# Splitting the natural-layout load of a linear-attention chunk, and moving the output's zero fill

## The chip, the cores and the metric

One Trainium2 chip, one of its cores. The metric is the device time of the kernel in microseconds (us), the median of several runs. The engines are TensorE (PE, with its weight loads as PEld), VectorE (DVE), ScalarE (ACT), GpSimd (POOL) and SyncE (SP); SP does no arithmetic and issues most of the DMAs, each when its turn in SP's queue has come and what it waits for has arrived.

## The reference

Three layers in a row, in float32. First a linear attention with a state per head (4 batches, 8 heads, 768 steps, 48 channels), then a dense layer pair on the 3072 tokens of 384 channels, then a mixture of 8 experts of which each token takes two:

```python
for t in range(S):
    cur = einsum('bhd,bhe->bhde', u * k_t, v_t)
    y[:, :, t] = einsum('bhd,bhde->bhe', r_t, state + cur)
    state = w_t[..., None] * state + einsum('bhd,bhe->bhde', k_t, v_t)
x = y as (3072, 384)
x = ((x @ w1) * (x @ w2)) @ w3 @ w_out
out = sum over the 2 best experts e: weight * (relu(x @ w1[e]) @ w2[e])
```

The term with u is, at each step and head, the sum over channels of r * k * u, times v.

## The kernel before, in words

The time axis is cut into 24 chunks of 128 steps, all eight heads at once. Each chunk has two inputs. dtc (772 KB, load_dt, line 177) holds r, k and w with channels on partitions. natc (640 KB, load_na, line 181) holds r, k and v with steps on partitions, r and k in the first 768 columns and v, padded, in the last 512. Both have two buffers, so the load for chunk j + 2 waits for the last reader of chunk j.

The thirteen steps of a chunk are the list STEPS (line 331). The ones that matter here: pre_u (line 217) makes rku = r*k*u from natc by two multiplies, on DVE for chunks 2 to 4 and on POOL for all others, into a single buffer; pre_c (line 224) sums it over the channels of a head on DVE (cc); pre_d (line 230) puts cc on a diagonal with eight ACT instructions (am); at_ov lays the products of chunk j over the rest of am; at_T turns k for the state; at_kv (line 257, from do_kv) adds k v to the state; at_y (line 278, from do_y) is the chunk's output on PE, which reads v from natc, and its two halves xh (ACT) and xl (DVE). y and the transposes of at_T share one PSUM bank (bY). After y of chunk j, do_y issues load_na(j + 2); after pre_r of chunk j, do_r issues load_dt(j + 2).

Two chunks make a group of 256 tokens, which then passes through the dense layers: mo_ab (line 486, eighteen matmuls of 256 columns a call), mo_x (line 510, twelve of 400) and mo_out. Matrices are split into a high and a low part, so each product is three matmuls (mm3, line 169). A group has 12 slots; at the end of each, run_todo issues the attention steps whose slot it is. The slots are written out by hand: chunk j takes them from WHEN (line 399) for j up to 5 and from 6j - 14 + LATE (line 405) after that. From chunk 6 on, y stands at slot 6j - 8, pre_u at 6j - 17, pre_r at 6j - 16, pre_c at 6j - 16 and pre_d at 6j - 15. Within one slot, instructions come in the order in which they were registered, loads of weights ahead of steps. Only DVE runs in the program's order; the framework orders the other engines' queues, SP's too, by its own modelled times, apart from instructions in keep_in_program_order, which stay behind what was traced before them on their engine.

At slot 14 fill_table (line 635) sets the routing table's slots to their start values by three stores of short rows and zeroes 896 rows of x2 in DRAM. At slots 24, 30, 36, 42 and 48 fill_out (line 646) zeroes one fifth of the output each, which the experts later add to by scatter.

In the slots below 0 the weights w3 and w_out are folded into one matrix (the prologue), beside the first steps of chunks 0 to 2. After the twelve groups come the eight experts, which this change doesn't touch; their loads and gathers begin in the last group.

Of the kernel before, what the change touches and what calls it, by code (L numbers as in the profile page):

```python
# [8 lines left out]
F32 = mybir.dt.float32  # L9
# [7 lines left out]
OP = mybir.AluOpType  # L17

P = 128
B, H, S, D = 4, 8, 768, 48  # L20
DM, FF, E = 384, 1024, 8
N = B * S
NCH = N // P
# [3 lines left out]
VW = 64  # L27
NDT = 8 * P + 8 * (HC + 1)
NNAT = 2 * DM + H * VW
# [8 lines left out]
NROW = N + DUMP  # L38
# [33 lines left out]
def tile_kernel(ctx: ExitStack, tc: tile.TileContext, dt, nat, w3t, wout, w1, w2, e1, e2, cf, ci, out):  # L72
    nc = tc.nc
    pe, act, dve, pool, sp = nc.tensor, nc.scalar, nc.vector, nc.gpsimd, nc.sync
# [15 lines left out]
    def c(n):  # L90
        o, w = CF[n]
        return cft[:, o:o + w]
# [21 lines left out]
    att = attx.enter_context(tc.tile_pool(name="att", bufs=2))  # L114
# [57 lines left out]
        pe.matmul(o, wl, xh, start=False, stop=stop)  # L172


    DT, NA, FG, RC, KT, RT, AM, KN, XH, XL, KS = ({} for _ in range(11))

    def load_dt(j):
        DT[j] = att.tile([P, NDT], F32, name="dtc")
        sp.dma_start(out=DT[j], in_=dt[j])

    def load_na(j):
        NA[j] = att.tile([P, NNAT], F32, name="natc")
        sp.dma_start(out=NA[j], in_=nat[j])

    def fgv(j):
        return FG[j].rearrange("p (a i) -> p a i", i=HC + 1)
# [6 lines left out]
    def pre_rec(j, step):  # L193

        fa = fgv(j)[:, :, 1:]
        if step == 0:
            RC[j] = att.tile([P, 8, HC], F32, name="rc", bufs=1)
            KT[j] = att.tile([P, 4, 2, HC], F32, name="kt")
            act.activation(out=RC[j], in_=fa, func=AF.Ln)
            act.activation(out=RC[j], in_=RC[j], func=AF.Exp, scale=-1.0)  # L200
        else:
            t = KT[j].rearrange("p a s i -> p (a s) i")
            dve.tensor_tensor(out=t, in0=fa, in1=RC[j], op=OP.mult)
            dve.scalar_tensor_tensor(RC[j], t, -2.0, RC[j], op0=OP.add, op1=OP.mult)
# [12 lines left out]
    def pre_u(j):  # L217
        t = att.tile([P, DM], F32, name="rku", bufs=1)
        on = dve if 2 <= j < 5 else pool
        on.tensor_tensor(out=t, in0=NA[j][:, :DM], in1=NA[j][:, DM:2 * DM], op=OP.mult)  # L220
        on.tensor_tensor(out=t, in0=t, in1=c("u"), op=OP.mult)
        KS["u", j] = t

# [28 lines left out]
        act.copy(out=KN[j].rearrange("p a t -> p (a t)"), in_=bY)  # L252

    def vv(j, h):
        return NA[j][:, 2 * DM + h * VW:2 * DM + (h + 1) * VW]

    def at_kv(j):
        kv = bK[:, :4 * D].rearrange("p (a e) -> p a e", a=4)
        for a in range(4):
            for hb in range(2):  # L260
                pe.matmul(kv[64 * hb:64 * hb + 64, a], KN[j][:, a, 64 * hb:64 * hb + 64],  # L261
                          vv(j, 2 * a + hb)[:, 16 * hb:16 * hb + D], start=True, stop=True,
                          tile_position=(0, 64 * hb))
        sc = att.tile([P, 4], F32, name="sc")
        dve.tensor_tensor(out=sc, in0=fgv(j)[:, 0::2, HC], in1=fgv(j + 1)[:, 1::2, HC], op=OP.mult)

        new = att.tile([P, 4, D], F32, name="snew", bufs=2)
        src = kv
        if j % CPB:
            src = att.tile([P, 4, D], F32, name="stmp", bufs=1)  # L270
            dve.tensor_tensor(out=src, in0=kv, in1=KS["s", j], op=OP.add)
        dve.tensor_tensor(out=new, in0=src, in1=sc[:, :, None].to_broadcast([P, 4, D]), op=OP.mult)
        KS["s", j + 1] = new
        for hb in range(2):
            q = slice(64 * hb, 64 * hb + D)
            act.copy(out=St[(j + 1) % 2][q, :, D * hb:D * hb + D], in_=new[q])

    def at_y(j):
        first = j % CPB == 0
        yv = bY[:, :3 * P].rearrange("p (k t) -> p k t", k=3)  # L280
        qs = []
        for q in range(4):
            lst = []
            for kb in range(3):
                a, b = PIECES[kb][q]
                if b is None:
                    hs, so = ((a, 32 * (a % 2)),), 64 * (a % 2)
                else:
                    hs, so = ((a, 32), (b, 0)), 32
                ms = [(vv(j, h)[:, o:o + 32], AM[j][:, h, :]) for h, o in hs]  # L290
                if not first:
                    ms.append((St[j % 2][:, a // 2, so:so + 32], RT[j][:, a // 2].rearrange("p s i -> p (s i)")))
                for i, (lt, rh) in enumerate(ms):
                    lst.append((yv[32 * q:32 * q + 32, kb], lt, rh, i == 0, i == len(ms) - 1, (0, 32 * q)))
            qs.append(lst)
        for i in range(max(map(len, qs))):
            for q in range(4):
                if i < len(qs[q]):
                    o, lt, rh, st, en, tp = qs[q][i]
                    pe.matmul(o, lt, rh, start=st, stop=en, tile_position=tp)  # L300
        g, s = divmod(j, 2)
        if s == 0:
            XH[g] = xp.tile([P, 3, 2 * P], F32R, name="xh")
            XL[g] = xp.tile([P, 3, 2 * P], F32R, name="xl")
        h, l = XH[g][:, :, s * P:s * P + P], XL[g][:, :, s * P:s * P + P]
        act.copy(out=h, in_=yv)  # L306
        dve.tensor_tensor(out=l, in0=yv, in1=f(h), op=OP.subtract)

    def do_y(j):
        at_y(j)  # L310
        if j + 2 < NCH:
            load_na(j + 2)

    def do_kv(j):
        if j % CPB < CPB - 1:
# [10 lines left out]
    def do_r(j):  # L326
        pre_r(j)
        if j + 2 < NCH:
            load_dt(j + 2)

    STEPS = (do_kv, do_y, at_A, do_ov, do_T, pre_scan, lambda j: pre_rec(j, 1), pre_k, do_r, lambda j: pre_rec(j, 0),
             pre_u, pre_c, pre_d)


    woh, wol = [w.rearrange("p (j d) -> p j d", d=XW) for w in (WBh, WBl)]
# [53 lines left out]
    SPG = 12  # L389
    todo = {}  # L390

    def at(slot, fn, *a):
        todo.setdefault(slot, []).append((fn, a))

    def run_todo(k):
        for fn, a in todo.pop(k, []):
# [1 line left out]

    WHEN = {0: (-13, -12, -14, -13, -14, -21, -18, -17, -17, -20, -19, -16, -14),
# [15 lines left out]
    for slot, fn, a in zip(LDA, (load_dt, load_na, load_dt, load_na), (0, 0, 1, 1)):  # L415
        at(slot, fn, a)
# [227 lines left out]
            out=x2d[:DUMP].rearrange("(a p) d -> p a d", p=P), in_=zeros[:, None, :].to_broadcast([P, NT, DM])))  # L644

    def fill_out(i):
        lo, hi = [k * (NROW // P) // 5 for k in (i, i + 1)]
        n = hi - lo
        tc.keep_in_program_order(sp.dma_start(
            out=out[lo * P:hi * P].rearrange("(a p) d -> p a d", p=P),  # L650
            in_=zeros[:, None, :].to_broadcast([P, n, DM])))
# [171 lines left out]
        gate_at(SPG * ((t0 + GB) // 2) + 3, t0, 1 + late,  # L823
                (9, 9, 9, 10, 10, 10, 11, 11) if late else (13, 14, 17, 17, 19, 20, 23, 23))
    at(SPG + 2, fill_table)
    for i in range(5):
        at(2 * SPG + 6 * i, fill_out, i)

    for g in range(NGRP):
        sub = [(mo_ab, g, 0, 0), (mo_ab, g, 0, 1), None, (mo_ab, g, 1, 0), (mo_ab, g, 1, 1), (mo_x, g, 0),  # L830
# [188 lines left out]
```

## Time and profile before

| what | value |
| --- | --- |
| median of 3 runs | 945.47 us (944.18 to 946.84) |
| the profiled execution | 945.79 us |
| its span, first to last instruction | 944.0 us |
| mean granted TensorE clock | 0.989 |
| TensorE busy | 96% of the span |
| VectorE, ScalarE, GpSimd busy | 49%, 45%, 35% |

How to read it: the span is what the rows below are laid out in, with times from its start. The prologue takes it to about 66 us, group 0 to about 113 us, the other groups to about 475 us, and the experts to the end. The granted clock is the share of TensorE's full rate of 2.4 GHz that the chip allowed. Idle time of an engine counts only if it holds up the one that bounds the stretch; who that is, the chain of waits shows: it goes from the last instruction back, at each step to what released it. A load's time to landing runs from its issue to its completion, with what it stood in line for.

### The profile page before, as it was taken

How to read it: one execution, taken by the hardware profiler on the slowest of the kernel's cores; microseconds unless marked ns; L12 is line 12 of the kernel's file. 1: busy time of each engine (PE TensorE's matmuls, PEld its weight loads, DVE VectorE, ACT ScalarE, POOL GpSimd, SP SyncE). 2: the span in 40 equal slices, each digit the busy share in tenths (PEclk: the TensorE clock that was granted, in tenths of full speed). 3: DMA queues.
4: the chain of work that ended last, by engine and by line, in shares of the span. 5: the costliest groups of instructions: out<-in, count | busy, mean ns of one | idle time of the engine just before them, and what ended most of it. 6: DMA issues, size and time to landing. Idle time of an engine off the chain costs nothing.

```text
span 944.0 us, 17811 instructions
## 1 busy us (share of the span) xinstructions
PE 909.2 (96%) x7235; PEld 843.2 (89%) x7235; DVE 461.1 (49%) x1126; ACT 422.3 (45%) x875; POOL 331.0 (35%) x267
## 2 busy tenths in 40 slices
PE   8998895999999999999999999999999999999994
PEld 6787795999999999999999989899898998989894
DVE  5888753676776866866344353231313223130320
ACT  6776533645546456455252343433424343332420
POOL 1100101023032132131414635655556564555412
PEclk9999997999999999999999999999999999999998
DMA  9944595565334244230140555335163532614112
GB/s 356 369 166 171 191 85 178 165 201 143 120 79 124 81 97 123 76 83 30 31 171 18 108 186 156 65 95 136 28 170 70 154 65 75 153 34 104 17 20 36
DMA packets 49180, 111.65 MB, mean 118 GB/s; under 512 B 17600, under 2 KB 32192, under 8 KB 49088
## 3 DMA queue, kind: packets, MB, share of 16 engines
q1 hardware_dynamic: 33472, 85.98, 29.4%
q0 software_dynamic: 12160, 19.72, 11.6%
q10 hardware_dynamic: 3456, 4.72, 1.4%
q8 instruction: 58, 0.95, 0.4%
q14 instruction: 34, 0.28, 0.1%
HBM read 88.12 MB, written 22.27 MB: 117 GB/s over the span
## 4 chain that ended last, share of the span: by engine, by line
PE 87%; DVE 4%; ACT 4%; DMA 2%; issue 1%; POOL 1%; POOLq 0%; SPq 0%; ACTq 0%; DVEq 0%
PE pb L170 26%; PE pb L171 25%; PE pb L172 25%; PE pb L300 3%; PE pb L240 2%; PE pb L726 2%; DMA natc<-nat 2%; PE pb L764 1%; PE pb L261 1%; ACT am L233 1%; PE pb L250 1%; ACT top L145 1%; DVE cvz L154 1%; DMA raw<-w 0%; DVE am L245 0%
## 5 line engine op out<-in xcount | busy, mean ns | idle before, releaser
L170 PE MATMUL pb<-XTh,WAh 128*128 128x512 f32 (+1 forms) x384 | 133.3, 348 | 0.0
L171 PE MATMUL pb<-XTl,WAh 128*128 128x512 f32 (+1 forms) x384 | 131.9, 343 | 0.0
L170 PE MATMUL pb<-WBh,HH 128*128 128x384 f32 x384 | 130.9, 341 | 0.0
L172 PE MATMUL pb<-XTh,WAl 128*128 128x512 f32 (+1 forms) x384 | 130.9, 343 | 0.0
L172 PE MATMUL pb<-WBh,HH 128*128 128x384 f32 x384 | 129.6, 337 | 0.0
L171 PE MATMUL pb<-WBl,HH 128*128 128x384 f32 x384 | 129.5, 337 | 0.0
L742 DVE SCALAR_TENSOR_TENSOR HH<-pb,HH 128x256 fp32r<-128x256 f32 (+1 forms) x128 | 71.3, 558 | 116.2 <-ACT HH L741 116.2
L769 POOL DMA_INDIRECT out<-ye,ti x56 | 87.2, 1557 | 107.4 <-ACT ye L759 94.2
L220 POOL TENSOR_TENSOR rku<-natc 128x384 f32<-128x384 f32 x21 | 23.8, 1134 | 275.0 <-DMA natc<-nat 243.7
L741 ACT ACTIVATE HH<-pb 128x256 fp32r<-128x256 f32 (+1 forms) x128 | 62.7, 491 | 125.2 <-PE pb L172 124.1
L170 PE MATMUL pb<-xh,WAh 128*128 128x256 f32 x288 | 82.1, 285 | 11.8 <-ACT xh L306 9.8
L759 ACT ACTIVATE ye<-pb,ti 128x384 f32<-128x384 f32 x48 | 27.9, 581 | 145.5 <-PE pb L172 129.7
L124 DVE TENSOR_TENSOR XTl<-pb,XTh 128x512 fp32r<-128x512 f32 (+1 forms) x48 | 25.3, 570 | 130.4 <-ACT XTh L123 130.3
L233 ACT ACTIVATE am<-cft,cc 128x128 f32<-128x128 f32 x192 | 61.3, 393 | 51.3 <-DVE cc L227 51.2
L170 PE MATMUL pb<-xh,WBh 128*128 128x256 f32 x288 | 81.4, 283 | 1.0 <-DVE pp L498 1.0
L172 PE MATMUL pb<-xh,WBl 128*128 128x256 f32 x288 | 81.4, 283 | 0.9 <-DVE WBl L161 0.9
L171 PE MATMUL pb<-xl,WAh 128*128 128x256 f32 x288 | 82.0, 285 | 0.0
L172 PE MATMUL pb<-xh,WAl 128*128 128x256 f32 x288 | 82.0, 285 | 0.0
L171 PE MATMUL pb<-xl,WBh 128*128 128x256 f32 x288 | 81.4, 283 | 0.0
L170 PEld LDWEIGHTS pb<-XTh,WAh 128*128 128x128 f32 x384 | 72.2, 188 | 9.6 <-DVE HH L742 1.5
L171 PEld LDWEIGHTS pb<-XTl,WAh 128*128 128x128 f32 x384 | 72.2, 188 | 8.0
L172 PEld LDWEIGHTS pb<-XTh,WAl 128*128 128x128 f32 x384 | 71.8, 188 | 8.2
(174 smaller groups left out, 2198.9 us busy)
## 6 DMA issues: line engine op xcount, KB each, us to landing
dtc<-dt SPq DMA_DIRECT2D x24, 772.0 KB, 4.9
natc<-nat SPq DMA_DIRECT2D x24, 640.0 KB, 4.6
raw<-e SPq DMA_DIRECT2D x18, 768.0 KB, 6.8
raww<-e SPq DMA_DIRECT2D x14, 768.0 KB, 4.4
rawf<-w3t SPq DMA_DIRECT2D x16, 512.0 KB, 7.1
raw<-w SPq DMA_DIRECT2D x8, 768.0 KB, 5.7
x_rows<-xo ACTq DMA_DIRECT2D x24, 192.0 KB, 3.0
out<-zeros SPq DMA_DIRECT2D x4, 1152.0 KB, 7.7
```

Source lines behind the costliest of these rows:

```text
L124: (on or dve).tensor_tensor(out=l, in0=src, in1=f(h), op=OP.subtract)
L170: pe.matmul(o, wh, xh, start=start, stop=False)
L171: pe.matmul(o, wh, xl, start=False, stop=False)
L172: pe.matmul(o, wl, xh, start=False, stop=stop)
L220: on.tensor_tensor(out=t, in0=NA[j][:, :DM], in1=NA[j][:, DM:2 * DM], op=OP.mult)
L233: act.activation(out=AM[j][:, h], in_=ident, func=AF.Copy, scale=KS["c", j][:, h:h + 1])
L240: pe.matmul(bST[hb][:, P * a:P * a + P], KT[j][q, a].rearrange("p s i -> p (s i)"), RT[j][q, a].rearrange("p s i -> p (s i)"), start=True, ...
L300: pe.matmul(o, lt, rh, start=st, stop=en, tile_position=tp)
L741: act.activation(out=Hh[hf][:, ff], in_=bank[:, :n], func=AF.Relu)
L742: dve.scalar_tensor_tensor(Hl[hf][:, ff], bank[:, :n], 0.0, f(Hh[hf][:, ff]), op0=OP.max, op1=OP.subtract)
L759: act.activation(out=y[:n], in_=bank[:n], func=AF.Copy, scale=wt)
L769: ins = pool.indirect_dma_start(out=out, out_offset=bass.IndirectOffsetOnAxis(ap=ti(e, j)[:, 0:1], axis=0), in_=y[:n], in_offset=None, com ...
```

## The change

natc becomes two tiles: nrk with r and k (384 KB), reloaded for chunk j + 2 behind pre_u of chunk j, and nv with v (256 KB), reloaded behind y as before. kv, y and T of chunk 2 come one slot later. The fill of the output is cut into ten pieces, at slots 36, 42, and so on to 90. The arithmetic is the same.

```diff
+    def load_rk(j):
+        RK[j] = att.tile([P, 2 * DM], F32, name="nrk")
+        sp.dma_start(out=RK[j], in_=nat[j][:, :2 * DM])
+
+    def load_v(j):
+        VV[j] = att.tile([P, H * VW], F32, name="nv")
+        sp.dma_start(out=VV[j], in_=nat[j][:, 2 * DM:])
+
     def load_na(j):
-        NA[j] = att.tile([P, NNAT], F32, name="natc")
-        sp.dma_start(out=NA[j], in_=nat[j])
+        load_rk(j)
+        load_v(j)
...
-        on.tensor_tensor(out=t, in0=NA[j][:, :DM], in1=NA[j][:, DM:2 * DM], op=OP.mult)
+        on.tensor_tensor(out=t, in0=RK[j][:, :DM], in1=RK[j][:, DM:], op=OP.mult)
...
     def vv(j, h):
-        return NA[j][:, 2 * DM + h * VW:2 * DM + (h + 1) * VW]
+        return VV[j][:, h * VW:(h + 1) * VW]
...
     def do_y(j):
         at_y(j)
         if j + 2 < NCH:
-            load_na(j + 2)
+            load_v(j + 2)
+
+    def do_u(j):
+        pre_u(j)
+        if j + 2 < NCH:
+            load_rk(j + 2)
...
-             pre_u, pre_c, pre_d)
+             do_u, pre_c, pre_d)
...
-            2: (6, 7, 4, 5, 5, -10, 1, 1, 1, -9, -4, 2, 2),
+            2: (7, 8, 4, 5, 6, -10, 1, 1, 1, -9, -4, 2, 2),
...
     def fill_out(i):
-        lo, hi = [k * (NROW // P) // 5 for k in (i, i + 1)]
+        lo, hi = [k * (NROW // P) // 10 for k in (i, i + 1)]
...
-    for i in range(5):
-        at(2 * SPG + 6 * i, fill_out, i)
+    for i in range(10):
+        at(3 * SPG + 6 * i, fill_out, i)
```

## Rows read from the trace of the kernel before

**Rows 1.** The page's first part: busy us (share of the span), instructions.
```profile
PE 909.2 (96%) x7235; PEld 843.2 (89%) x7235; DVE 461.1 (49%) x1126; ACT 422.3 (45%) x875; POOL 331.0 (35%) x267
```

**Rows 2.** Table by stretches: length; PE, PEld, DVE, ACT, POOL busy; clock; DMA share; GB/s.
```profile
145.49:155.49 10.00, 0.16 (x2) 0.00 (x1) 1.26 (x3) 3.81 (x11) 3.98 (x4) 0.66 0.75 298
...
155.49:159.47 3.98, 3.97 (x19) 3.68 (x20) 3.98 (x6) 1.26 (x2) 0.00 (x0) 0.57 0.00 0
...
129.50:131.68 2.18, 2.18 (x21) 2.18 (x19) 2.18 (x5) 1.27 (x2) 0.00 (x0) 1.00 1.34 24
...
161.62:337.00 175.38, 175.38 (x1889) 170.13 (x1887) 123.56 (x339) 93.80 (x215) 40.76 (x38) 1.00 0.43 127
```

**Rows 3.** The chain of waits, 129 to 175 us: start, length, what.
```profile
133.75 15.06 DMA natc<-nat
148.95 1.00 POOL rku L220
...
151.04 0.56 DVE cc L227
...
155.06 0.38 ACT xh L306
```

**Rows 4.** The timeline of SP's queue, 105 to 172 us: start, length of issue.
```profile
123.83 7.93 SPq L640 DMA_DIRECT2D slots<-cit  x3
...
133.75 2.30 SPq L183 DMA_DIRECT2D natc<-nat  x1
136.87 0.37 SPq L179 DMA_DIRECT2D dtc<-dt  x1
```

**Rows 5.** DMA issues at 133 to 137 us, then all: size, us to landing (median).
```profile
natc<-nat SPq DMA_DIRECT2D x1, 640.0 KB, 15.1
...
dtc<-dt SPq DMA_DIRECT2D x1, 772.0 KB, 13.8
...
dtc<-dt SPq DMA_DIRECT2D x24, 772.0 KB, 4.9
natc<-nat SPq DMA_DIRECT2D x24, 640.0 KB, 4.6
...
x_rows<-xo ACTq DMA_DIRECT2D x24, 192.0 KB, 3.0
```

**Rows 6.** The timeline of DVE, 62 to 128 us: chunk 4's rku, chunk 5's cc.
```profile
111.00 0.55 DVE L220 TENSOR_TENSOR rku<-natc 128x384 f32<-128x384 f32 x1
...
123.33 0.55 DVE L227 TENSOR_REDUCE cc<-rku 128x8 f32<-128x384 f32 x1
```

**Rows 7.** The chain of waits over the span: kv of chunks 6, 12 and 18.
```profile
168.73 0.60 PE pb L261 x16
...
269.23 0.60 PE pb L261 x16
...
369.65 0.60 PE pb L261 x16
```

**Rows 8.** The timeline of SP's queue, 0 to 440 us: first and last zero fill.
```profile
142.68 0.73 SPq L649 DMA_DIRECT2D out<-zeros  x1
...
221.69 1.44 SPq L649 DMA_DIRECT2D out<-zeros  x1
```

**Rows 9.** Group 0: DVE's timeline (brackets: idle before, releaser), then the chain.
```profile
100.33 0.56 DVE L307 TENSOR_TENSOR xl<-pb,xh 128x384 fp32r<-128x384 f32 x1 [2.18 <-ACT xh L306]
...
71.70 3.92 DMA raw<-w
```

**Rows 10.** Timelines of POOL, SP, DVE; POOL's waits 160 to 430 us (total, times, longest).
```profile
191.59 1.15 POOL L220 TENSOR_TENSOR rku<-natc 128x384 f32<-128x384 f32 x1 [14.31 <-DMA natc<-nat]
...
199.34 0.33 SPq L179 DMA_DIRECT2D dtc<-dt  x1
...
222.49 1.23 DVE L190 TENSOR_TENSOR_SCAN fg<-dtc,d 128x520 f32<-128x520 f32 x1
...
POOL slots L629 <- DVE LZ L521: 14.9, 4, 3.9
```

More of the change, by code (lines that the diff above doesn't have):

```diff
@@ L172, in mm3 @@
         pe.matmul(o, wl, xh, start=False, stop=stop)
-    DT, NA, FG, RC, KT, RT, AM, KN, XH, XL, KS = ({} for _ in range(11))
+    DT, RK, VV, FG, RC, KT, RT, AM, KN, XH, XL, KS = ({} for _ in range(12))
     def load_dt(j):
```

## The prediction, made before the change was run

> **What bounds the kernel now.** The page's first part comes first: TensorE is busy 909.2 of 944.0 us of the span, so only time in which it stands still, or runs at a lower clock, can be won without less arithmetic [rows 1]. The table by stretches then shows where that is. From 161.62 to 337.00 us PE is busy for 175.38 of 175.38 us: the steady groups of chunks are bound by their matmuls, and nothing done there to a load can help. From 145.49 to 155.49 us it does nothing at all, with 10.00 us lost, and from 155.49 to 159.47 us the granted clock is 0.57, so mostly the lower level of 1.2 GHz, for eighteen matmuls (one call of mo_ab) that need 2.18 us at the full clock [rows 2]. The chain of waits says what ended last there: the natc load of chunk 6 takes the chain from 133.75 to 148.81 us; then rku on POOL at 148.95, cc on DVE at 151.04, and xh on ACT at 155.06, which lets PE start at 155.49 [rows 3]. xh is the cast of chunk 5's y, long computed; ScalarE takes its instructions in order, and chunk 6's am, which needs cc, stands in front.
>
> Why that load is late is read on SP's own queue. It belongs behind y of chunk 4 (slot 16), but the table fill of slot 14 comes first: three small-row stores whose issue takes 7.93 us from 123.83, then a zero fill. So natc is issued at 133.75, and dtc of chunk 8 at 136.87 [rows 4]. Behind that fill natc took 15.1 us to land and dtc 13.8, where the median of all natc loads is 4.6 [rows 5].
>
> **The change part by part.** *The reload of r and k.* Chunk 6's r and k no longer wait for y(4). They are asked for when chunk 4's first r*k multiply has read its tile; that multiply runs on DVE at 111.00 us and takes 0.55 [rows 6]. So the load can be issued near 111.6, 12 us ahead of the table fill at 123.83, and is in by 116.2 at the median of 4.6 us. Chunk 6's multiplies on POOL then wait only for their single rku buffer, free when cc(5) has read it: 123.33 + 0.55 = 123.88 [rows 6]. Two multiplies of 1.0 us [rows 3] give rku(6) at 126, and cc(6) comes at its own place in DVE's order, behind the r products of chunk 6 that SP's 136.87 load shows done [rows 4], so at about 137. PE then reaches 145.49 with ac, ph and xh ready, as in every later group. The stall of 10.00 us goes, and with no idle ahead of it mo_ab takes 2.18 instead of 3.98: 1.80 more. Sum: 11.8 us.
>
> *What is late next.* The v half of chunk 6 still stands behind the table fill. At worst it lands when natc did, 148.81 [rows 3]. Its first reader is kv(6), at 168.73 before [rows 7] and 11.8 earlier afterwards, at 156.9: 8.1 us of room. dtc(8), in at 150.7 [rows 4, 5], is read six slots after scan(7), after 156 as well. Neither ends last.
>
> *The other chunks.* Everywhere else r and k come about twelve slots earlier; no PE time hangs on it, since PE is full there [rows 2]. It covers the work twice over: where POOL waited for natc, it now waits for rku alone.
>
> *More DMAs.* 24 loads become 48 and five fills ten, 29 more issues at about 0.35 us (the issue of dtc in [rows 4] took 0.37): some 10 us on SP's queue, spread over 300 us in which that queue mostly waits for others. Cost 0; if the cover were gone it would be 0.4 us per chunk. In landing time, a store of 192 KB takes 3.0 us and a load of 640 KB 4.6 [rows 5], a line of about 2.3 us and 0.36 us for each 100 KB: 384 KB land in 3.7 us, 256 KB in 3.2, one after the other 6.9 instead of 4.6. Both halves are asked for some twelve slots (33 us) ahead, so this is covered. The Trainium skill (DMA: Bandwidth & Descriptors, "Rules for kernel authors") speaks against the split: for bandwidth it wants 128 partitions and at least 1 MiB per DMA. Taken as the limit here, that rule would add time for each split load, where the rows say that the whole of it is hidden; it is the fourth rival below.
>
> *The zero fill.* Five pieces start between 142.68 and 221.69 us or just behind [rows 8]. The steady pattern repeats every three groups, so kv(6), kv(12) and kv(18) can be compared: 168.73 to 269.23 is 100.50 us with four of the fills in it, 269.23 to 369.65 is 100.42 with none [rows 7]. The fill costs 0.08 us where it stands, so moving it gains and costs 0. The last piece now comes at slot 90, near 330 us, far before the experts' first scatter into out. One fill did stand right behind natc(7) at 142.68 [rows 8]; with it gone the traffic around 145 us is lighter, which is on the side of v(6).
>
> *Chunk 2's kv, y and T one slot later.* This lies in group 0, where DVE and ACT set the pace. The trace doesn't show that order, so I bound it. For a gain: DVE stood 2.18 us for chunk 2's xh ahead of xl [rows 9], and putting xl one slot back may fill that. For a loss: a slot, 2.18 us as mo_ab's [rows 2], because T(3) shares y's PSUM bank and comes next. The two are equally far, so I take 0.
>
> *Early loads in group 0 and the prologue.* rk(4) is ready to go when chunk 2's multiply (slot -4, on DVE) has read its tile, close to the weight load which the chain shows at 71.70 and which ACT waits for [rows 9]. If it goes in front, 384 KB by the slope above delay that weight by 1.4 us; if behind, nothing. On the other side the natc loads that used to share this stretch are smaller. I take 0, the row of the weight load being DVE's doing, not the queue's.
>
> Sum: 944.0 - 11.8 = 932.2 us of span. The profiled execution took 945.8 with what lies around it, so 934.0; it stands 0.3 above the median of 945.47, which makes **933.7 us**.
>
> **The rivals.** *First, a shorter wait in the old place.* v(6) or dtc(8) becomes what ends last. Against it stand 8.1 us of room; for it, that the fill's landing times are the longest in the trace [rows 5]. If v(6) needed twice 15.1 us it would land at 163.9, 7 us late: 940.7. Chance 0.05.
>
> *Second, the change doesn't do what it says.* The order on SP is not the program's: the framework orders that queue by its own modelled times. If it put rk(6) behind the table fill, it would be issued at 133.75 and land at the old time: 945.5. Against it: its release, 111.6, is 12 us ahead of that of the fill, which is tied behind dtc(7). Chance 0.03.
>
> *Third, slower: SP held by POOL.* load_rk(j + 2) waits in SP's queue for POOL's multiply of chunk j, and dtc(j + 2) stands behind it. The place is each steady chunk. For chunk 9 the multiply ran at 191.59, dtc(11) was issued at 199.34, and its scan read it at 222.49 [rows 10]. The load has 23.2 - 4.9 = 18.2 us of room (4.9 is dtc's median [rows 5]), and the multiply 7.7 us before it holds SP: PE feels it once POOL is 26 us late. Waits of POOL for routing work reach 3.9 us [rows 10], so it would need several such in a row. Where it happened, each us beyond that point is paid at each of the 16 steady chunks; 2 us would give 933.7 + 32 = 965.7. Chance 0.03.
>
> *Fourth, the split loads set the pace.* If each chunk paid the 2.3 us by which two loads take longer than one, 24 chunks would give 55 us, so 988.9. The rows hide 6.9 us under 33. Chance 0.01. This is the case by the 1 MiB rule of the Trainium skill, same page and section.
>
> **How the numbers follow.** Forecast 0.88, rivals 0.05, 0.03, 0.03 and 0.01. A measurement of this kernel tells about 0.3%, 2.8 us, from no change: below 942.6 is faster, above 948.3 slower. Faster: 0.88 and 0.04 of the first rival, 0.92. Same: 0.03 and the rest of the first, 0.04. Slower: 0.03 + 0.01 = 0.04. The range takes in group 0's 2.2 us either way, the 1.4 us of the weight load on the upper side, and 1.3 us by which the runs shown lie off their median: 933.7 - 3.5 gives 930.2, 933.7 + 4.9 gives 938.6; I put the lower end at 929.5, since all of group 0 waits on others and may gain a little more.
>
> **What would show it.** After: nrk of chunk 6 issued near 112 us on SP, ahead of the table fill; no natural-layout load in the chain of waits; no gap on PE at 145 us, and the granted clock 1.00 through 130 to 170 us; kv(6) near 157 us; three groups still 100.4 to 100.5 us; fills from about 180 us on, without a mark on PE. I am wrong if the gap is there with another releaser, if group 0 (up to 113 us) is longer or shorter by over 3 us, or if dtc is issued late in the steady groups.

## The result, and the profile after

The changed kernel takes 935.71 us (935.50 to 936.07, 4 runs) where the kernel before takes 946.15 us on the same chip (944.18 to 948.83, 4 runs): a ratio of 0.9888, with a 95% interval of 0.9863 to 0.9914. The forecast was 933.7 us, with a range of 929.5 to 938.6. So the sign and the range hold, and the number is 2.0 us short. The profiled span fell from 944.0 to 933.6 us.

First the page of the changed kernel: the busy times, which answer to [rows 1], and the DMA issues with their median time to landing, which answer to [rows 5].

```profile
PE 905.8 (97%) x7235; PEld 842.0 (90%) x7235; DVE 447.8 (48%) x1126; ACT 423.4 (45%) x875; POOL 330.4 (35%) x267
...
nrk<-nat SPq DMA_DIRECT2D x24, 384.0 KB, 5.2
...
nv<-nat SPq DMA_DIRECT2D x24, 256.0 KB, 3.4
...
out<-zeros SPq DMA_DIRECT2D x9, 576.0 KB, 4.5
```

Of the 10.4 us that left the span, PE's busy time (909.2 and 905.8) accounts for 3.4; the other 7.0 are time in which it stood still. Next the timeline of SP's queue in the changed kernel (start, length of issue), which answers to [rows 4] and [rows 8].

```profile
112.03 2.98 SPq L183 DMA_DIRECT2D nrk<-nat  x2
125.08 0.33 SPq L179 DMA_DIRECT2D dtc<-dt  x1
125.45 8.14 SPq L653 DMA_DIRECT2D slots<-cit  x3
133.64 1.78 SPq L656 DMA_DIRECT2D x_rows<-zeros  x1
135.53 1.96 SPq L187 DMA_DIRECT2D nv<-nat  x1
...
177.36 0.43 SPq L662 DMA_DIRECT2D out<-zeros  x1
...
328.95 0.43 SPq L662 DMA_DIRECT2D out<-zeros  x1
```

r and k of chunk 6 are asked for at 112.03 us, 13.4 us ahead of the table fill at 125.45; only v still stands behind it, at 135.53. The next two views are the table by stretches (length; PE, PEld, DVE, ACT, POOL busy; granted clock; DMA share; GB/s) and the chain of waits, which answer to [rows 2] and [rows 7].

```profile
144.00:170.00 26.00, 26.00 (x242) 25.36 (x241) 17.65 (x50) 14.75 (x30) 2.04 (x2) 1.00 0.48 173
200.00:325.00 125.00, 125.00 (x1337) 121.43 (x1336) 79.93 (x235) 64.94 (x147) 30.45 (x30) 1.00 0.43 129
```

```profile
72.65 5.43 DMA raw<-w
...
125.57 0.60 PE pb L269 x16
...
158.52 0.60 PE pb L269 x16
...
259.01 0.60 PE pb L269 x16
...
359.44 0.60 PE pb L269 x16
```

PE is busy for all of 144 to 170 us at the full clock, where it had stood still for 10.00 us and then run at 0.57 [rows 2]. No natural-layout load is left in the chain. In the chain of the kernel before, kv of chunk 4 stands here (kv of chunk 6 is in [rows 7]):

```profile
123.94 0.60 PE pb L261 x16
```

From kv of chunk 4 to kv of chunk 6 the kernel before took 168.73 - 123.94 = 44.79 us, and this one takes 158.52 - 125.57 = 32.95: 11.84 us went here. Yet the whole gain of these two profiled spans is 10.4, and kv of chunk 4 comes 1.6 us later than before. Something ahead of it costs time.

### The profile page after: what moved, and what is told of

Its sections match the earlier page's. It is cut to its first block, busy times and chain, and to the rows that moved or that the text cites. A ratio compares the mean times of both kernels' runs of the same rounds, so it can differ in the third digit from the quotient of the medians.

```text
span 933.6 us, 17851 instructions
## 1 busy us (share of the span) xinstructions
PE 905.8 (97%) x7235; PEld 842.0 (90%) x7235; DVE 447.8 (48%) x1126; ACT 423.4 (45%) x875; POOL 330.4 (35%) x267
## 4 chain that ended last, share of the span: by engine, by line
PE 87%; DVE 6%; ACT 3%; DMA 1%; issue 1%; POOL 0%; ACTq 0%; POOLq 0%; SPq 0%; DVEq 0%
PE pb L170 26%; PE pb L171 25%; PE pb L172 25%; PE pb L308 4%; PE pb L248 2%; PE pb L739 2%; PE pb L777 1%; PE pb L269 1%; PE pb L258 1%; DVE cvz L154 1%; ACT top L145 1%; DMA raw<-w 1%; ACT am L241 1%; DMA raw<-e 0%; PE pb L374 0%
## 5 line engine op out<-in xcount | busy, mean ns | idle before, releaser
L642 POOL DMA_INDIRECT slots<-g_sc,g_si x48 | 52.4, 1091 | 159.4 <-DVE g_si L641 82.4
L228 POOL TENSOR_TENSOR rku<-nrk 128x384 f32<-128x384 f32 x21 | 21.9, 1041 | 184.1 <-DVE cc L235 79.8
```

Of the source, the lines that this page charges most:

```text
L228: on.tensor_tensor(out=t, in0=RK[j][:, :DM], in1=RK[j][:, DM:], op=OP.mult)
L642: ins = pool.indirect_dma_start(out=table, out_offset=bass.IndirectOffsetOnAxis(ap=si[:, i, k:k + 1], axis=0), in_=SC[:, i, k, :], in_offs ...
```

## The experiments

The runs stand in three sets, each set on one chip beside the kernel before, whose median was 945.99, 948.70 and 945.61 us. The profiled executions also differ by up to 4 us in their first 60 us, for one and the same kernel by up to 2, so the table measures between landmarks of each run's own trace, at their starts in the chain of waits: the weight load that the chain crosses (raw<-w), y of chunk 1, and kv of chunks 4 and 6. (In "reload tied behind y" the chain does not pass kv of chunk 4, which is taken from PE's timeline.) "Prologue" is the time from the start of the first to the start of the last of the six conversions (top, L145) that ScalarE makes before it casts that y. From kv of chunk 6 to the end, the second set's four kernels take 778.5 to 780.1 us, all others 775.1 to 775.6; so the second set's times are set against the others' only by their ratios.

| kernel | median us | ratio (95%) | prologue | weight load | y(1) to kv(4) | kv(4) to kv(6) |
| --- | --- | --- | --- | --- | --- | --- |
| before | 946.15 | | 7.72 | 3.92 | 60.80 | 44.79 |
| after | 935.71 | 0.9888 (0.9863 to 0.9914) | 9.22 | 5.43 | 61.47 | 32.95 |
| reload called behind y | 935.27 | 0.9883 (0.9850 to 0.9916) | 7.73 | 5.62 | 62.06 | 32.98 |
| old zero fill | 936.77 | 0.9901 (0.9877 to 0.9926) | 9.24 | 5.55 | 61.54 | 32.98 |
| old slots of chunk 2 | 938.44 | 0.9923 (0.9895 to 0.9951) | 9.22 | 5.35 | 63.40 | 32.95 |
| moved call, chunks up to 5 | 935.62 | 0.9878 (0.9852 to 0.9905) | 7.70 | 5.75 | 61.87 | 32.98 |
| reload tied behind y | 948.38 | 0.9989 (0.9969 to 1.0009) | 7.71 | 4.39 | 59.2 | 45.6 |
| before, table fill later | 937.29 | 0.9868 (0.9836 to 0.9900) | 7.71 | 4.23 | 61.18 | 32.97 |
| tied up to chunk 5 | 936.38 | 0.9868 (0.9836 to 0.9901) | 7.72 | 4.37 | 59.19 | 32.98 |
| all multiplies on POOL | 939.23 | 0.9893 (0.9863 to 0.9924) | 9.65 | 4.12 | 59.69 | 32.96 |
| before, table later and slots | 932.07 | 0.9850 (0.9827 to 0.9873) | 7.72 | 4.24 | 59.08 | 32.96 |
| after, again | 937.00 | 0.9904 (0.9883 to 0.9925) | 9.21 | 5.13 | 61.11 | 32.98 |
| tied up to chunk 5, again | 932.99 | 0.9852 (0.9829 to 0.9876) | 7.70 | 4.19 | 59.00 | 32.98 |
| before, table later, again | 934.58 | 0.9874 (0.9848 to 0.9901) | 7.70 | 4.13 | 60.98 | 32.97 |

**First set: undo one part.** The theory is that the own tile of r and k moves the load ahead of the table fill, and that this is the gain.

*The reload's call behind y again:*

```diff
     def do_y(j):
         at_y(j)
         if j + 2 < NCH:
+            load_rk(j + 2)
             load_v(j + 2)
     def do_u(j):
         pre_u(j)
-        if j + 2 < NCH:
-            load_rk(j + 2)
```

> r and k keep their own tile, but are reloaded behind y again; the fill in ten pieces and chunk 2's slots stay as in the changed kernel. If the gain is the place of this load ahead of the table fill, PE's gap of 10 us near 145 us is back, with the half-clock mo_ab behind it: 935.7 + 11.8 = 947.5, less up to 1.7 us which group 0 gets back because chunks 2 to 5 no longer load early, so 945.5 to 947.5. If the gain came from the smaller tiles or from the zero fill leaving the stretch around 142 us, the gap stays away and the time stays within 934 to 937.

It didn't undo anything: 935.27 us, kv(4) to kv(6) 32.98. The trace has chunk 6's reload at 112.39 us on SP, still ahead of the fill. This looks as if the framework put SP's queue in order by when a transfer's tile comes free, since the multiply frees nrk wherever the call stands. On that reading it is the separate tile that moves the load; in any case the place of the call is not a way to move it back.

*The zero fill as it was, five pieces from slot 24; then chunk 2's kv, y and T at their old slots:*

```diff
-        lo, hi = [k * (NROW // P) // 10 for k in (i, i + 1)]
+        lo, hi = [k * (NROW // P) // 5 for k in (i, i + 1)]
...
-    for i in range(10):
-        at(3 * SPG + 6 * i, fill_out, i)
+    for i in range(5):
+        at(2 * SPG + 6 * i, fill_out, i)
```

> The changed kernel with the old zero fill, five pieces from slot 24. If the fill is worth nothing where it stands, as kv(6) to kv(12) against kv(12) to kv(18) said: 935.7, within 0.5 us. If its first piece behind nv of chunk 7 lengthens the queue at 143 us so far that nv of chunk 6 or dtc of chunk 8 comes late, a gap on PE near 150 us and 2 to 10 us more.

```diff
-            2: (7, 8, 4, 5, 6, -10, 1, 1, 1, -9, -4, 2, 2),
+            2: (6, 7, 4, 5, 5, -10, 1, 1, 1, -9, -4, 2, 2),
```

> The changed kernel with chunk 2's kv, y and T back on slots 6, 7 and 5. In the changed kernel group 0 ran 2.5 us late at ov of chunk 2 (94.33 against 91.87) and only 0.4 us late at pp (110.84 against 110.40). If the slots won these 2 us back, 937.7 and pp near 113; if the stretch would have caught up in any case, 935.7 within 0.5 us; if the later slots cost time, 933.5 to 935.

The old zero fill changes nothing where the fill stands: 32.98 against 32.95 us to kv(6), and 775.4 against 775.1 from there to the end. Its 1.1 us against the changed kernel lie within the two intervals. The old slots cost 63.40 - 61.47 = 1.93 us, all of it between y(1) and kv(4); the time is higher too (938.44), with intervals that overlap. DVE's timeline shows where: its wait for xh ahead of chunk 2's xl (the bracket) is 2.19 us with the old slots, as in [rows 9], and 1.06 with the new; and its next wait, 0.83 us for rc ahead of kt, is there only with the old. Together that is 1.96 us. First the run with the old slots, then the changed kernel.

```profile
102.39 0.56 DVE L315 TENSOR_TENSOR xl<-pb,xh 128x384 fp32r<-128x384 f32 x1 [2.19 <-ACT xh L314]
...
105.50 0.69 DVE L211 TENSOR_TENSOR kt<-fg,rc 128x512 f32<-128x512 f32 x1 [0.83 <-ACT rc L208]
```

```profile
103.36 0.56 DVE L315 TENSOR_TENSOR xl<-pb,xh 128x384 fp32r<-128x384 f32 x1 [1.06 <-ACT xh L314]
103.90 0.69 DVE L211 TENSOR_TENSOR kt<-fg,rc 128x512 f32<-128x512 f32 x1
```

*The early reload only from chunk 6 on, by moving the calls for the others:*

```diff
     def do_y(j):
         at_y(j)
         if j + 2 < NCH:
+            if j + 2 < 6:
+                load_rk(j + 2)
             load_v(j + 2)
     def do_u(j):
         pre_u(j)
-        if j + 2 < NCH:
+        if 6 <= j + 2 < NCH:
             load_rk(j + 2)
```

> The changed kernel with the early reload from chunk 6 on only; r and k of chunks 2 to 5 are loaded behind y, with v. If the early loads of chunks 2 to 5 are what made group 0 late (the weight load behind nrk of chunk 4 took 5.43 us where it took 3.92, and ScalarE's order at 57 us put a weight split ahead of the fold), xl of chunk 1 comes a us earlier, PE's gap ahead of the first mo_ab is 1.5 us instead of 3.1, and the time is 934.0. If the lateness comes from chunk 2's slots, or from POOL's multiply beside DVE at 113 us, it stays at 935.7.

It fails as a test for the same reason as the first: the weight load still takes 5.75 us, so chunk 4's reload still went in beside it. It shows, though, that PE stands still for this load: its timeline has an idle stretch of 2.92 us right behind it.

```profile
80.82 0.55 PE L170 MATMUL pb<-xh,WBh 128*128 128x256 f32 x1 [2.92 <-ACT WAh L156]
```

**Second set: order SP by hand.** The reload is now tied in program order (keep_in_program_order), behind y and so behind the table fill, for all chunks:

```diff
-    def load_rk(j):
+    def load_rk(j, pin=False):
         RK[j] = att.tile([P, 2 * DM], F32, name="nrk")
-        sp.dma_start(out=RK[j], in_=nat[j][:, :2 * DM])
+        ins = sp.dma_start(out=RK[j], in_=nat[j][:, :2 * DM])
+        if pin:
+            tc.keep_in_program_order(ins)
...
             load_v(j + 2)
+            load_rk(j + 2, True)
```

> As the changed kernel, but the reload of r and k stands behind y and is tied behind v's load on SP, so for chunk 6 it comes after the table fill again, tile of its own or not. If what gained is that this load no longer stands behind the fill, PE's gap of 10 us near 146 us is back, kv(4) to kv(6) is 44.9 us instead of 33.0, and the time 945 to 948. If the gap went away for another reason (smaller loads, lighter traffic, the zero fill moved), kv(4) to kv(6) stays at 33 to 36 us and the time at 934 to 938.

The gain is gone: 948.38 against 948.70 us, with every other part of the change still in. SP's timeline, the chain and PE's timeline of that run show the old stall in its old place:

```profile
122.39 7.91 SPq L654 DMA_DIRECT2D slots<-cit  x3
130.35 2.33 SPq L657 DMA_DIRECT2D x_rows<-zeros  x1
132.79 2.14 SPq L189 DMA_DIRECT2D nv<-nat  x1
134.98 1.22 SPq L183 DMA_DIRECT2D nrk<-nat  x1
```

```profile
134.98 12.39 DMA nrk<-nat
147.50 1.00 POOL rku L230
...
153.62 0.38 ACT xh L316
```

```profile
154.04 0.58 PE L170 MATMUL pb<-xh,WAh 128*128 128x256 f32 x1 [9.82 <-ACT xh L316]
```

*The other way round: the kernel before, with nothing but the table fill three slots later*, behind the natc load of chunk 6:

```diff
-    at(SPG + 2, fill_table)
+    at(SPG + 5, fill_table)
```

> The kernel before with one number changed: the table fill at slot 17 in place of 14, so behind the load for chunk 6. No split, no moved zero fill, no moved slots. If the order of two DMAs on SP's queue is the whole cause, the load for chunk 6 is issued near 126 us and lands in 4 to 6 us, the gap near 145 us is gone, and the time is 933 to 936, unless the load for chunk 7, now the one behind the fill, is late in its turn (landing after 152 us, read at 151): then a wait of 1 to 6 us and 935 to 941. If the split is what is needed, it stays at 944 to 947.

One number does what the whole change does: ratio 0.9868 (0.9836 to 0.9900), kv(4) to kv(6) 32.97 us. SP's timeline of that run:

```profile
128.92 0.33 SPq L183 DMA_DIRECT2D natc<-nat  x1
129.30 7.67 SPq L640 DMA_DIRECT2D slots<-cit  x3
```

The load was expected on the queue near 126 us and went out at 128.92, still ahead of the fill. These two runs show the cause from both sides: it is the order of this one load and the table fill. The split isn't needed for it.

*The changed kernel with the reloads of chunks 2 to 5 tied behind y as above, the others early:*

```diff
             load_v(j + 2)
+            if j + 2 < 6:
+                load_rk(j + 2, True)
...
-        if j + 2 < NCH:
+        if 6 <= j + 2 < NCH:
             load_rk(j + 2)
```

> The changed kernel with r and k of chunks 2 to 5 tied behind v's load, from chunk 6 on early. If nrk of chunk 4 standing next to the weight load is what made that load slow (5.4 us instead of 3.9), the weight lands in 3.9 again, and y(1) to kv(4) is 1.4 us shorter than the changed kernel's 61.5: 60.0 us, time 934.2. If the weight load is slow for another reason, 61.5 us and 935.7.

*And the changed kernel with all of the r*k*u multiplies on POOL:*

```diff
-        on = dve if 2 <= j < 5 else pool
+        on = pool
```

> The changed kernel with r*k*u of chunks 2 to 4 on POOL as well (six DVE instructions of 0.55 us less, 3.3 us, in the stretch where DVE sets the pace). With r and k there early, POOL can do it long ahead, and nrk of chunk 4 is then asked for near 53 us, away from the weight load at 72. If DVE's time and that weight load are what bind group 0, y(1) to kv(4) falls from 61.5 to 57.5 to 60 us and the time to 932 to 934.5. If DVE instructions beside POOL's multiplies grow by as much (0.16 became 0.98 at 113 us), 935 to 936.5.

Tying chunks 2 to 5 takes the weight load back to 4.37 us and the prologue to 7.72, and makes y(1) to kv(4) 2.3 us shorter than in the changed kernel; the time was left open by intervals that overlap. With all multiplies on POOL, chunk 4's reload is issued at 55.95 us, well ahead of the weight load at 71.41, which then takes 4.12 us; y(1) to kv(4) is 59.69, 1.8 less than in the changed kernel. The time shows none of it (939.23; the ratio's interval overlaps the changed kernel's). The prologue, at 9.65 us the longest of all, takes back 0.4. The profiled execution was the quickest of the four, 937.04 against 939.12 to 939.37, so no trace shows where the rest went.

**Third set: side by side.** The changed kernel, the one tied up to chunk 5, and the kernel before with its table fill moved, alone and together with chunk 2's new slots:

```diff
-            2: (6, 7, 4, 5, 5, -10, 1, 1, 1, -9, -4, 2, 2),
+            2: (7, 8, 4, 5, 6, -10, 1, 1, 1, -9, -4, 2, 2),
...
-    at(SPG + 2, fill_table)
+    at(SPG + 5, fill_table)
```

> The kernel before with two numbers' worth of change: the table fill three slots later, as in the run of that alone, and chunk 2's kv, y and T a slot later; one tile of natural layout, the old zero fill. By the theory that the load ahead of the fill is worth 11.9 us and the slots 1.9 us, and that the early reload beside the weight load costs 1.5 us, this has both gains without the cost: first y to kv of chunk 4 some 59.3 us (61.47 in the changed kernel, 61.18 with the table alone), kv of 4 to kv of 6 32.97, and a time some 14 us under the kernel before, 1.5 to 2 us under the changed kernel on the same chip. By the rival that the slots only win beside the new tile: first y to kv of chunk 4 stays at 61.2 and the time is that of the run with the table alone.

> The changed kernel itself, run beside the other three of this set on one chip: a ratio near 0.988 to the kernel before, first y to kv of chunk 4 at 61.5 us, with the weight load at 5.4 us behind the reload of r and k. If the 1.5 us at the weight load is real, it stands 1 to 2 us above the next one.

> The changed kernel with the reload of r and k of chunks 2 to 5 kept in its old place behind v's, and that of chunks 6 on where the change puts it, run again beside the changed kernel: first y to kv of chunk 4 at 59.2 us, 2.3 us shorter than the changed kernel's, kv of 4 to kv of 6 at 32.98, and a time 1 to 2 us under the changed kernel's. If the difference lies in the start of each execution and not in the reload, the two times are the same within 0.5 us.

> The kernel before with nothing but the table fill three slots later, again, beside the changed kernel: kv of 4 to kv of 6 at 32.97 us. By the theory that all of the gain is the order of that one load and the fill, its time is the changed kernel's within 1 us, the slots' 1.9 us against it and the early reload's 1.5 us for it.

The kernel before with a moved table fill and three moved slots, one tile and the old zero fill, takes 932.07 us, 4.9 us less than the changed kernel beside it, where 1.5 to 2 were expected; the intervals of their ratios (0.9827 to 0.9873, and 0.9883 to 0.9925) don't meet. It beats both kernels. The one tied up to chunk 5 takes 932.99, 4.0 us less than the changed kernel, where 1 to 2 were expected, and its interval (0.9829 to 0.9876) is also apart. The slots' gain comes again without the split: 60.98 - 59.08 = 1.90 us, and 934.58 - 932.07 = 2.5 in the time, where the intervals overlap. The table fill alone was expected within 1 us of the changed kernel; it is 2.4 below, with intervals that overlap. What these misses have in common is the early reload, which costs more than the 1.5 us written there.

What the early reload of chunks 2 to 5 costs is read by laying the changed kernel beside the one tied up to chunk 5 (again): y(1) starts at 64.10 in the one, at 64.09 in the other, so rows can be compared as they stand. First DVE's, then POOL's timeline of the changed kernel.

```profile
112.62 0.55 DVE L235 TENSOR_REDUCE cc<-rku 128x8 f32<-128x384 f32 x1
...
113.69 0.98 DVE L273 TENSOR_TENSOR sc<-fg 128x4 f32<-128x4 f32 x1
114.59 0.34 DVE L279 TENSOR_TENSOR stmp<-pb,snew 128x192 f32<-128x192 f32 x1
114.97 0.97 DVE L280 TENSOR_TENSOR snew<-stmp,sc 128x192 f32<-128x192 f32 x1
115.87 0.55 DVE L315 TENSOR_TENSOR xl<-pb,xh 128x384 fp32r<-128x384 f32 x1
```

```profile
113.31 1.33 POOL L228 TENSOR_TENSOR rku<-nrk 128x384 f32<-128x384 f32 x1 [43.47 <-DVE cc L235]
114.72 1.01 POOL L229 TENSOR_TENSOR rku<-rku,cft 128x384 f32<-128x384 f32 x1
```

And the same of the kernel tied up to chunk 5, with its weight load in the chain.

```profile
111.33 0.55 DVE L237 TENSOR_REDUCE cc<-rku 128x8 f32<-128x384 f32 x1
...
112.39 0.16 DVE L275 TENSOR_TENSOR sc<-fg 128x4 f32<-128x4 f32 x1
112.47 0.35 DVE L281 TENSOR_TENSOR stmp<-pb,snew 128x192 f32<-128x192 f32 x1
112.85 0.36 DVE L282 TENSOR_TENSOR snew<-stmp,sc 128x192 f32<-128x192 f32 x1
113.13 0.55 DVE L317 TENSOR_TENSOR xl<-pb,xh 128x384 fp32r<-128x384 f32 x1
```

```profile
114.00 1.64 POOL L230 TENSOR_TENSOR rku<-nrk 128x384 f32<-128x384 f32 x1 [44.17 <-DMA nrk<-nat]
```

```profile
72.64 4.19 DMA raw<-w
```

SP's timeline of the changed kernel shows chunk 4's reload right in front of that weight load; in the other it went out at 65.96.

```profile
71.59 0.33 SPq L183 DMA_DIRECT2D nrk<-nat  x1
72.65 4.29 SPq L166 DMA_DIRECT2D raw<-w  x2
```

The weight load starts at 72.65 and 72.64 and takes 5.43 and 4.19: 1.24 us. The difference stays at that up to cc of chunk 4 (112.62 and 111.33: 1.29). Then it doubles: with r and k of chunk 5 already there, POOL starts its multiply as soon as cc frees the buffer, at 113.31, and DVE's two short products beside it take 0.98 and 0.97 us instead of 0.16 and 0.36. xl is 2.74 us later, and kv(4) 2.47 (61.47 and 59.00 from y(1)). Where POOL started at 114.00, those products were over.

A third part lies ahead of y(1). ScalarE's timeline of the changed kernel, and then of the one tied up to chunk 5:

```profile
54.67 0.78 ACT L145 ACTIVATE top<-rawf 128x512 f16<-128x512 bf16 x1
...
56.81 0.63 ACT L145 ACTIVATE top<-raw 128x384 f16<-128x384 bf16 x1
...
57.82 0.78 ACT L145 ACTIVATE top<-rawf 128x512 f16<-128x512 bf16 x1
...
63.47 0.52 ACT L156 CAST WAh<-cvz 128x384 fp32r<-128x384 f32 x1 [0.98 <-DVE cvz L154]
63.89 0.65 ACT L145 ACTIVATE top<-raw 128x384 f16<-128x384 bf16 x1
```

```profile
56.28 0.78 ACT L145 ACTIVATE top<-rawf 128x512 f16<-128x512 bf16 x1
...
57.90 0.78 ACT L145 ACTIVATE top<-rawf 128x512 f16<-128x512 bf16 x1
...
59.04 0.64 ACT L145 ACTIVATE top<-raw 128x384 f16<-128x384 bf16 x1
...
63.98 0.64 ACT L145 ACTIVATE top<-raw 128x384 f16<-128x384 bf16 x1
```

With the reload called behind the multiply, the framework orders the weight conversions another way: a raw one goes ahead of the last rawf one, DVE's products come late for ScalarE, and the stretch takes 9.22 us instead of 7.70. The table has 9.2 or more in each kernel with that call for the early chunks, and 7.7 in each without it. Why the order turns out so was not tried. Nor is all of the 1.5 us shown to reach the time: the two kernels with a moved call have the early reload and the short prologue, and from the first of the six conversions to kv(4) they take 69.76 and 69.71 us where the changed kernel takes 70.90, so 1.1 to 1.2; their times, 935.27 and 935.62 us, don't stand apart from 935.71.

## Why the prediction was right, and where it was 2.0 us off

- **The stall of 10.00 us and the half clock behind it, 11.8 us: right.** Measured 11.84, from kv(4) to kv(6), and shown by taking it away (tied) and by getting it without the split (table fill later).
- **What is late next, nothing: right.** v of chunk 6 went out at 135.53 and landed 12.2 us later, at 147.7; PE has no idle time up to its reader, kv(6) at 158.52. dtc of chunk 8 wasn't felt either. Rival 1 didn't come.
- **More DMAs, 0: right.** Three steady groups take 100.49 us (158.52 to 259.01) and 100.43 (259.01 to 359.44), against 100.50 and 100.42 [rows 7]. A half of r and k takes 5.2 us to land, where the line drawn through [rows 5] gave 3.7, and PE doesn't notice. The Trainium skill (DMA: Bandwidth & Descriptors, "Rules for kernel authors") wants at least 1 MiB per DMA for bandwidth; loads of 384 and 256 KB cost nothing in these groups, so this stage doesn't wait on bandwidth. Rival 4 didn't come.
- **SP held by POOL: no.** In the steady chunks dtc goes out on time (at 155.71 us, for one, ahead of nrk at 157.27), and PE is busy for 125.00 of 125.00 us from 200 on. POOL's waits did change, though: its multiplies, free of natc, now wait for DVE's routing work instead, up to 15.3 us at a time, and the routing waits that reached 3.9 us [rows 10] reach 11.7. The prediction's "waits for rku alone" was too simple.
- **The zero fill, 0: right.** SP's timeline has all ten pieces, from 177.36 to 328.95 (the page's nine are those of 576 KB), and none leaves a mark on PE.
- **Chunk 2's slots, taken as 0 between -2.18 and +2.18: mis-sized.** They won 1.93 us (1.90 in the other kernel). The favourable bound named the right row: DVE's wait of 2.18 us ahead of xl [rows 9], which fell to 1.06; the rest is the next wait, 0.83 us for rc, which went away.
- **Early loads in group 0 and the prologue, taken as 0 between 0 and 1.4: this is the step that failed.** The reason given was that the weight load in the chain was DVE's doing. DVE does release it, but its length of 3.92 is transfer time, and rk(4) in front made it 5.43: 1.5 more than before, 1.24 more than with the reload tied back. The upper bound, worked out as the slope's 1.4, was the value to take. Two costs weren't in the sum at all: DVE's short products beside POOL's earlier multiply (about 1.2 us) and the turned order in the prologue (1.1 to 1.5).

Put together: 933.7 - 1.9 + 1.2 + 1.2 + 1.5 = 935.7 us, which is what was measured. That it meets the median to a tenth is luck: the prologue's share is not known to better than 0.4 us, and the kernel before itself moved from 945.47 us (3 runs) to 946.15 (4 runs). The terms that were taken as 0 or left out had opposite signs, gaining 1.9 and costing up to 3.9, so the range held by more than it deserved.

## What to carry to other kernels

When one stall accounts for the gain, ask which two transfers stand in the wrong order, and try to swap those two alone: here two kinds of slot numbers gave 932.07 us where a new tile gave 937.00. A load that comes earlier is not free while the pipeline fills: it can lengthen the load that the start waits for, and it releases another engine into a stretch where that engine gets in the way. Test an order by what the trace shows as issued, since moving a call may move nothing.

## What was not expected of the hardware

Two short DVE instructions grew beside a POOL multiply: 128x4 from 0.16 to 0.98 us, 128x192 from 0.36 to 0.97. The first ended at 114.67 and POOL's first multiply at 114.64; the second at 115.94 and POOL's second at 115.73. The one between them, stmp, kept its 0.34. The Trainium skill (SBUF — State Buffer, "SBUF: two separate sides") says that VectorE with two SBUF inputs and a GpSimd instruction that reads SBUF exclude each other for a whole instruction. The trace agrees: sc and snew read SBUF alone, stmp reads one input from PSUM. No run was made to test this reason.

The steady groups show the same meeting, the other way round. In the kernel before, kt<-dtc,fg (128x256, both inputs in SBUF) takes 0.42 us, but 1.25 to 1.84 in six of 17 times, each beside POOL's second multiply. In the changed kernel the multiplies come earlier, none of the 17 meets one, and all take 0.42 to 0.43. The busy time of all of VectorE follows: 445.7 to 448.5 us in the nine kernels in which r and k of the steady chunks come early, 461.1 to 464.2 in the five in which they come behind y, split or not. So the early reload gives VectorE some 15 us, which are worth nothing here because PE is full.

In the changed kernel PE stood still for 3.15 us ahead of group 0's first mo_ab, where it was 1.51 in the kernel tied up to chunk 5 (again), and the granted clock over 66 to 76 us was 0.83, so partly the lower level of 1.2 GHz, instead of 1.00. No cost of it shows, since the chain there runs through DVE and the weight load.

The three short-row stores of the table fill held SP's queue for 7.67 to 8.68 us in every kernel, wherever they stood. The fill was only ever moved as a whole, so no run separates these stores from the zero fill behind them. In the kernel before, the last two of them land 16.9 and 14.9 us after their issue, at 141.2 and 143.6 us, the zero fill at 146.4 and natc at 148.8.
